# Values applied in one burst per group and tile, three rotating PSUM banks for exponentials and sums, a later tanh, and another order of the first y products

## The chip, the cores and the metric

The kernel runs on one core of a Trainium2 chip. The metric is the device time of one execution in microseconds (us). TensorE is called PE, its weight loads PEld, VectorE DVE, ScalarE ACT, GpSimd POOL; SyncE (SP) issues the transfers.

## The reference

Two blocks read the same `x` (2048 rows of 512): sliding-window attention with 32 heads of 16 and a window of 256, and a feed-forward block of width 1792 with a tanh gelu. A sigmoid gate mixes them row by row.

```python
g = _sigmoid((x * gate_w).sum(-1, keepdims=True))
# a: q, k, v = x @ wqkv; mask: 0 <= i - j < 256
p = _softmax(jnp.where(mask, (q @ k.T) * Dh ** -0.5, -1e9))
a = (p @ v) @ wo
# b
h = _gelu(x @ w1 + b1)
b = h @ w2 + b2
return g * a + (1 - g) * b
```

## The kernel before, in words

**Dense work.** The rows are cut into four tiles of 512 (T, NT = 4), each into four blocks of 128 (NB). Every dense product is done three times in fp32r (`mm3`, L94): high by high, high by low, low by high, with numbers split into a high part (rounded) and a low part (the rest). `qkv(t)` (L280) makes queries, keys and values of a tile and stores them in DRAM (SQ, SK, SV). `mlp(n)` (L569) is one of eight turns over half of the hidden width (`half`) and one tile: seven `u` products (12 matmuls each), `gelu` (L542) on each, then four `y` products (one per block, 21 matmuls each). Half 0 adds `b2` and stores into YA; half 1 reads YA back through the tile `ya` and stores into YB. `final(t)` (L631) multiplies by `wo` and mixes with the gate.

`gelu` has seven steps on a 128x512 tile: two ACT passes on `u` in PSUM, which give x1 = u + b1 and its square; f2 on DVE, the argument of tanh (L552); f3 on ACT, tanh (L555); f4 on DVE (L558); f5 on DVE, the high part of h (L561); f6 on POOL, the low part of h (L564). A `y` product's third matmul (L97) is the one that reads the low part. The tiles `x1` and `sq` have two buffers each.

**Attention.** Heads are taken in 8 groups of four (NG), keys in 16 blocks of 128 (NKB). A unit `u` is one key block of one group: 128 units. Three steps per head run beside each other:

- `att_max` (L374): scores `sm` of a query block, whose row maximum is taken by DVE (tile `jm`, L388), 8 units ahead (LEAD). `att_rows` (L394) turns the maxima of four blocks into two extra rows of `qs`, through the tiles `nm` and `tt`, with four POOL copies (`put`, L408).
- `att_exp` (L414): scores `st` of a key block against its up to 384 queries, in PSUM (two banks); ACT writes the exponentials into a tile `pt` (L435, 11 buffers, two heads each), POOL zeroes what the mask forbids (`sel`, L427 and L430).
- `att_pv` (L441): the values of a key block times those exponentials are added into the PSUM bank `pv` of a query tile `c`. A value operand is 32 columns wide, so the four heads of a group stand side by side in the array (`tile_position`, L455). It is in plain fp32, each of these matmuls being two instructions in the records. `att_pvs` (L473) calls it after every odd key block: for the two blocks done last, and after the second block of a tile also for the last two of the tile before, which reach into this tile. That makes two bursts per group and tile. After the second, ACT copies `pv` out as `nd` (L466), and it goes to DRAM.

`att_norm` (L485) then, for every second group, reads the denominators (`den`) and numerators (`num`) back, takes the reciprocal (`rec`, L496), spreads it through DRAM (`rb`) and multiplies (L501).

**What sets the order.** On PE, ACT, DVE and POOL the instructions stand as the program emits them (`MANUAL`), and every engine works through its own in that order. The program keeps a planned clock: `tick(ns)` advances it, `after(ns, f)` puts a step on a list that `tick` empties when it is due, `need` brings due steps forward. The main loop goes through the units; per head it emits, as `ORDER` says, `sm`, `st`, at the third head (PVAT) the `att_pvs` of the unit before, and then `fill`, which emits dense work worth STEP / 4 of planned time. So a `u` or `y` matmul group stands between two pairs of score matmuls. `GELU` lists the planned delays of f1 to f6, `NORM` the step of `att_norm`. Transfers all go through SP, whose order a scheduler chooses; SP waits in order as well.

A tile with a tag takes the next of that tag's `bufs` buffers, and its first writer waits until the last reader of the tile that was there is done.

Of the kernel before, what the change touches and what calls it, by code (L numbers as in the profile page):

```python
# [18 lines left out]
T = 512  # L19
# [13 lines left out]
def gated_mix(ctx: ExitStack, tc: tile.TileContext, x, wqkv, wo, w1, b1, w2, b2, gate_w, out):  # L33
# [35 lines left out]
    b2b = cp.tile([128, D], F32, name="b2b")  # L69
# [15 lines left out]
    nms = [cp.tile([128, RB, 32], F32R, name=f"nm{i}") for i in range(2)]  # L85
    for nm in nms:
        nc.gpsimd.memset(f32(nm), 0.0)
# [38 lines left out]
    def load_raw(key, early=False):  # L126
        kind, i = key
        src = {"qk": lambda: wk4[:, :, i * 128:(i + 1) * 128],
               "v": lambda: wqkv[i * 128:(i + 1) * 128, 2 * D:3 * D],
               "w1": lambda: w1k[:, :, i * 128:(i + 1) * 128],  # L130
               "w2": lambda: w2[i * 128:(i + 1) * 128],
               "wo": lambda: wo[i * 128:(i + 1) * 128]}[kind]()
        if early and kind == "v" and i < 2:
            raw = sb.tile([128, T], F32, tag="sq", bufs=2, name=f"raw_{kind}{i}")
        elif early and kind == "v":
            raw = f32(sb.tile([128, 2, T], F32R, tag="h", bufs=8, name=f"raw_{kind}{i}"))[:, 0]
        elif early:
            raw = sb.tile([128, 2, 384], F32, tag="pt", bufs=11, name=f"raw_{kind}{i}")
# [46 lines left out]
    def load_xr(t):  # L185
        for b in range(NB):
            xrs[t, b] = sb.tile([128, D], F32, tag="tmp", bufs=4, name=f"xr{t}_{b}")
            nc.sync.dma_start(xrs[t, b], x[t * T + b * 128:t * T + (b + 1) * 128])
# [38 lines left out]
    def gate_z(t, b):  # L227
        xr = xrs.pop((t, b))
        junk = sb.tile([128, D], BF16, tag="x1", bufs=2, name=f"xj{t}_{b}")
        nb = t * NB + b  # L230
        nc.vector.tensor_tensor_reduce(junk, xr, gwb, 1.0, 0.0, ALU.mult, ALU.add, z[:, nb:nb + 1])
# [48 lines left out]
    def qkv(t):  # L280
# [17 lines left out]
        for n, (kind, j) in enumerate(pieces):  # L298
# [9 lines left out]
            if t == 0 and n == 10:  # L308
                nc.sync.dma_start(b2b, b2.partition_broadcast(128))
                nc.sync.dma_start(b1c, b1.rearrange("(f p) -> p f", p=128))  # L310
# [83 lines left out]
    def att_rows(g_, rb):  # L394

        need(*[("max", g_, rb * RB + b, i) for b in range(RB) for i in range(4)])
        m = Ms.pop((g_, rb))
        nm = nms[rb % 2][:, :, 0:8].rearrange("p b (i k) -> p k b i", k=2)
# [3 lines left out]
        tt = sb.tile([128, RB, 32], F32, tag="tt", bufs=2, name=f"tt{g_}_{rb}")  # L402
        nc.vector.transpose(tt.rearrange("p b c -> p (b c)"), f32(nms[rb % 2]).rearrange("p b c -> p (b c)"))

        def put(i):
            dst = qs[96:104, :, rb * RB * 128:(rb + 1) * RB * 128]
            dst = dst.rearrange("r s (b i j) -> r s b i j", b=RB, i=4)[:, :, :, i]
            nc.gpsimd.tensor_copy(dst, tt[32 * i:32 * i + 8].unsqueeze(1).broadcast_to([8, 2, RB, 32]))  # L408
            if i == 3:
                done.add(("rows", g_, rb))  # L410
        for i in range(4):
            after(PUT * (i + 1), put, i)

    def att_exp(g_, kb, i):  # L414
# [3 lines left out]
        if s == 0:  # L418
            pts[g_, kb, pr] = sb.tile([128, 2, 384], F32, tag="pt", bufs=11, name=f"pt{g_}_{kb}_{pr}")
# [21 lines left out]
    def att_pv(g_, kb, c):  # L441
# [6 lines left out]
        if first:  # L448
# [3 lines left out]
            pvs[g_, c] = ps.tile([128, T], F32, tag="pv", bufs=1, name=f"pv{g_}_{c}")  # L452
# [7 lines left out]
        tick((e - q) * 1.67 + 150)  # L460
        if kb % NB == NB - 1 and c == kb // NB:
            nd = sb.tile([128, T], F32, tag="tmp", bufs=4, name=f"nd{g_}_{c}")
# [22 lines left out]
    def att_norm(t, c):  # L485
# [3 lines left out]
        rec = sb.tile([128, 32], F32, tag="rec", bufs=2, name=f"rec{t}_{c}")  # L489
        nc.sync.dma_start(den, v[:, 16, :].rearrange("i (j c) -> i j c", c=32))  # L490
        num = sb.tile([128, T], F32, tag="tmp", bufs=4, name=f"num{t}_{c}")
        rb = sb.tile([128, T], F32, tag="tmp", bufs=4, name=f"rb{t}_{c}")
        nc.sync.dma_start(num, v[:, 0:16, :])

        def rcp():
            nc.vector.reciprocal(rec, den)  # L496
            nc.sync.dma_start(RD[t][c].rearrange("h (j c) -> (h j) c", c=32), rec)
# [17 lines left out]
    def load_o(t):  # L515
# [7 lines left out]
        for c in range(NC):  # L523
            need(("o", t, c))
            if t == 0:
                raw = sb.tile([128, T], F32, tag=("x1", "sq")[c % 2], bufs=2, name=f"or{t}_{c}")
            else:
                raw = sb.tile([128, 2, 384], F32, tag="pt", bufs=11, name=f"or{t}_{c}")
# [40 lines left out]
    def mlp(n):  # L569
# [22 lines left out]
        for b in range(NB):  # L592
            ts = slice(b * 128, (b + 1) * 128)
            if n + 1 == len(TURNS) and b == 2:
                load_o(0)
            p = ps.tile([128, D], F32, tag="d", bufs=2, name=f"y{t}_{half}{b}")
            if half == 1:
                ya = sb.tile([128, D], F32, tag="ya", bufs=2, name=f"ya{t}_{b}")
                need(("y", 0, t, b))
                nc.sync.dma_start(ya, YA[t][ts])  # L600
            for i in range(HF):
                need(hs[i].name, ("w", ("w2", half * HF + i)))
                w = wt["w2", half * HF + i]
                mm3(p, hs[i][:, 0, ts], hs[i][:, 1, ts], w[:, 0], w[:, 1], i == 0, i == HF - 1)
                yield MM3
                if last and b == NB - 1 and later:
                    load(later.pop(0))
            def ev(p=p, b=b, ts=ts, ya=b2b if half == 0 else ya):
                y = sb.tile([128, D], F32, tag="y", bufs=1, name=f"yo{t}_{half}{b}")
                nc.vector.scalar_tensor_tensor(y, p, 0.5, ya, op0=ALU.mult, op1=ALU.add)  # L610
                nc.sync.dma_start((YA, YB)[half][t][ts], y)
                done.add(("y", half, t, b))
            after(100, ev)
# [17 lines left out]
    def final(t):  # L631
# [8 lines left out]
        for b in range(NB):  # L640
# [3 lines left out]
            a = sb.tile([128, 2, 384], F32, tag="pt", bufs=11, name=f"ao{nb}")  # L644
# [52 lines left out]
    for u in range(-LEAD, NU):  # L697
# [17 lines left out]
        if u % NB == 2 and -NB < u < NU - NB:  # L715
            att_load_v(*divmod(u // NB + 1, NT))
# [17 lines left out]
NORM = 6000  # L734
GELU = (700, 1500, 2300, 3300, 4200, 5000)
# [29 lines left out]
```

## Time and profile before

| | |
|---|---|
| runs | 807.09 us median of 3 (806.85 to 811.15) |
| profiled execution | 806.06 us, of which span 804.4 us |
| PE busy | 783.4 us, 97% |
| DVE, ACT, POOL busy | 526.3, 427.0, 357.9 us |
| `pv` matmuls (L455) | 1408 records, 91.4 us busy |
| `st`, `sm` matmuls | 172.2, 169.5 us busy |
| mean granted PE clock | 0.998 |
| transfers | 135.72 MB, 52.5% of 16 engines' time |

A matmul's record begins when it starts and ends when its last row is through; matmuls follow each other before that, so the distance from start to start says what one costs, and the busy times of neighbours overlap. An engine's waits are listed with the instruction that released it. In the rows, `L455` is line 455 of the kernel, `128x384` the partitions and elements of the operand, `x16` a run of 16 such records in one row.

### The profile page before, as it was taken

How to read it: one execution, taken by the hardware profiler on the slowest of the kernel's cores; microseconds unless marked ns; L12 is line 12 of the kernel's file. 1: busy time of each engine (PE TensorE's matmuls, PEld its weight loads, DVE VectorE, ACT ScalarE, POOL GpSimd, SP SyncE). 2: the span in 40 equal slices, each digit the busy share in tenths (PEclk: the TensorE clock that was granted, in tenths of full speed). 3: DMA queues.
4: the chain of work that ended last, by engine and by line, in shares of the span. 5: the costliest groups of instructions: out<-in, count | busy, mean ns of one | idle time of the engine just before them, and what ended most of it. 6: DMA issues, size and time to landing. Idle time of an engine off the chain costs nothing.

```text
span 804.4 us, 14522 instructions
## 1 busy us (share of the span) xinstructions
PE 783.4 (97%) x4630; PEld 612.9 (76%) x4630; DVE 526.3 (65%) x1517; ACT 427.0 (53%) x865; POOL 357.9 (44%) x702
## 2 busy tenths in 40 slices
PE   9999999989999999999999999999999999999988
PEld 6888888866777777777767867877787778776767
DVE  4532333997478757956895798568767966891353
ACT  4433423365467446745674576456646654775631
POOL 2200000156357544854674477437645753675100
PEclk9999999999999999999999999999999999999999
DMA  9985856636332544462235546432664374345863
GB/s 259 390 313 197 307 176 196 207 114 237 105 101 68 195 141 120 147 194 86 78 108 158 170 126 218 119 97 90 195 193 125 103 227 153 99 128 177 282 234 117
DMA packets 94925, 135.72 MB, mean 169 GB/s; under 512 B 32256, under 2 KB 43776, under 8 KB 94848
## 3 DMA queue, kind: packets, MB, share of 16 engines
q1 hardware_dynamic: 94848, 134.79, 52.5%
q8 instruction: 37, 0.61, 0.3%
q14 instruction: 40, 0.33, 0.1%
HBM read 79.70 MB, written 55.05 MB: 168 GB/s over the span
## 4 chain that ended last, share of the span: by engine, by line
PE 75%; DVE 12%; issue 4%; ACT 4%; POOL 3%; DMA 2%; SPq 0%; DVEq 0%; POOLq 0%; ACTq 0%
PE pv L455 9%; PE st L423 8%; PE sm L383 7%; PE y L95 6%; PE y L97 6%; PE y L96 5%; DVE jm L388 4%; PE u L95 4%; PE qk L95 4%; PE qk L97 4%; PE qk L96 4%; PE u L96 3%; PE u L97 3%; DVE sqh L552 2%; PE v L95 2%
## 5 line engine op out<-in xcount | busy, mean ns | idle before, releaser
L388 DVE CUSTOM_DVE_ANT_0 jm<-sm,mask 128x384 bf16<-128x384 f32 (+2 forms) x512 | 269.7, 527 | 129.7 <-PE sm L383 106.5
L435 ACT ACTIVATE pt<-st 128x384 f32<-128x384 f32 (+2 forms) x512 | 232.2, 471 | 194.8 <-PE st L423 189.6
L427 POOL TENSOR_SCALAR_AFFINE_SELECT pt<-pt 128x256 f32<-128x256 f32 x256 | 120.9, 472 | 203.9 <-ACT pt L435 199.3
L423 PE MATMUL st<-qs,ks 128*128 128x384 f32 (+2 forms) x512 | 172.2, 338 | 8.5 <-ACT pt L435 5.6
L383 PE MATMUL sm<-ks,qs 96*128 96x384 f32 (+2 forms) x512 | 169.5, 333 | 4.2 <-DVE M L388 4.0
L423 PEld LDWEIGHTS st<-qs,ks 128*128 128x128 f32 x512 | 97.2, 190 | 36.7 <-ACT pt L435 14.1
L383 PEld LDWEIGHTS sm<-ks,qs 96*128 96x128 f32 x512 | 96.4, 188 | 30.4 <-DVE M L388 8.9
L430 POOL TENSOR_SCALAR_AFFINE_SELECT pt<-pt 128x256 f32<-128x256 f32 x224 | 101.9, 455 | 0.0
L564 POOL TENSOR_TENSOR h<-x1h,h 128x512 fp32r<-128x512 f32 x56 | 75.4, 1346 | 42.3 <-DVE h L561 38.6
L455 PE MATMUL pv<-pt,vbuf 128*32 128x384 f32 (+2 forms) x1408 | 91.4, 388 | 0.1
L95 PE MATMUL y<-w,h 128*128 128x512 f32 x224 | 90.9, 406 | 0.0
L97 PE MATMUL y<-w,h 128*128 128x512 f32 x224 | 88.1, 393 | 0.9 <-POOL h L564 0.9
L96 PE MATMUL y<-w,h 128*128 128x512 f32 x224 | 87.8, 392 | 0.0
L408 POOL CAST qs<-tt 8x256 fp32r<-8x256 f32 x128 | 60.5, 473 | 50.5 <-PE u L97 39.2
L95 PE MATMUL u<-mx,w 128*128 128x512 f32 x196 | 80.5, 411 | 0.0
L96 PE MATMUL u<-mx,w 128*128 128x512 f32 x196 | 76.8, 392 | 0.0
L97 PE MATMUL u<-mx,w 128*128 128x512 f32 x196 | 76.6, 391 | 0.0
L455 PEld LDWEIGHTS pv<-pt,vbuf 128*32 128x32 f32 x1408 | 38.3, 109 | 36.9 <-issue 17.2
L555 ACT ACTIVATE sqh<-sqh 128x512 f32<-128x512 f32 x56 | 35.3, 631 | 46.5 <-DVE sqh L552 46.2
L552 DVE SCALAR_TENSOR_TENSOR sqh<-sqh,x1h 128x512 f32<-128x512 f32 x56 | 53.0, 946 | 2.3 <-ACT sqh L549 1.6
L250 DVE TENSOR_TENSOR qke<-qk,qke 128x512 fp32r<-128x512 f32 x32 | 22.1, 690 | 49.5 <-ACT qke L247 45.4
L95 PEld LDWEIGHTS y<-w,h 128*128 128x128 f32 x224 | 42.4, 189 | 11.8 <-issue 11.1
(118 smaller groups left out, 1186.2 us busy)
## 6 DMA issues: line engine op xcount, KB each, us to landing
mx<-XT SPq DMA_DIRECT2D x24, 512.0 KB
SQ<-qke SPq DMA_DIRECT2D x16, 512.0 KB
SK<-qke SPq DMA_DIRECT2D x16, 512.0 KB
qs<-SQ SPq DMA_DIRECT2D x64, 128.0 KB
ND<-nd SPq DMA_DIRECT2D x32, 256.0 KB
ks<-SK SPq DMA_DIRECT2D x60, 128.0 KB
raw_w<-in_B_w_dram SPq DMA_DIRECT2D x28, 256.0 KB
SV<-vx SPq DMA_DIRECT2D x16, 272.0 KB
```

Source lines behind the costliest of these rows:

```text
L95: nc.tensor.matmul(p, lh, rh, start=first, stop=False)
L96: nc.tensor.matmul(p, lh, rl, start=False, stop=False)
L97: nc.tensor.matmul(p, ll, rh, start=False, stop=last)
L383: nc.tensor.matmul(p[:, :w], qs[0:96, pr, b * 128:(b + 1) * 128], ks[0:96, pr, s, k0:k0 + w], start=True, stop=True)
L388: nc.vector.tensor_tensor_reduce(junk[:, :w], p[:, :w], mask[:, 384 - w:384], 1.0, -3e38, ALU.add, ALU.max, M[:, b % RB, i:i + 1])
L423: nc.tensor.matmul(p[:, :w], ks[:, pr, s, kb * 128:(kb + 1) * 128], qs[:, pr, kb * 128:kb * 128 + w], start=True, stop=True)
L427: nc.gpsimd.affine_select(out=pt[:, :, 0:128], in_=pt[:, :, 0:128], pattern=[[0, 2], [1, 128]], compare_op=ALU.is_ge, fill=0.0, base=0, ch ...
L430: nc.gpsimd.affine_select(out=pt[:, :, 256:384], in_=pt[:, :, 256:384], pattern=[[0, 2], [-1, 128]], compare_op=ALU.is_ge, fill=0.0, base= ...
L435: nc.scalar.activation(pt[:, s, :w], p[:, :w], AF.Exp, scale=SCALE)
L455: nc.tensor.matmul(pv[32 * i:32 * i + 32, q - c * T:e - c * T], vt[:, 68 * (kb % NB) + 17 * i:68 * (kb % NB) + 17 * i + 32], pts[g_, kb, i ...
L552: nc.vector.scalar_tensor_tensor(sq, sq, GC, x1, op0=ALU.add, op1=ALU.mult)
L564: nc.gpsimd.tensor_sub(h[:, 1], x1, f32(h[:, 0]))
```

## The change

1. `att_pvs` works once per group and tile, after the tile's last key block: on the six blocks that reach into the tile (four for the first tile). `pt` has 14 buffers, and a tile's values are fetched at the start of its first unit's turn and not two units earlier.
2. `pv` has no bank of its own. It takes one of three banks under the tag `st`, in turn with the scores. The planned cost of a value block falls from 1.67 ns per column and 150 to 0.8 and 40.
3. `GELU` puts f3 (tanh) at 3600 instead of 2300, and f4, f5, f6 at 4600, 5500 and 6800 instead of 3300, 4200 and 5000. `NORM` is 4500 instead of 6000.
4. The `y` products of the first two blocks are interleaved: six of block 0, three of block 1 (YSWAP), the last of block 0, the other four of block 1.
5. Buffers: `b2` is not kept but loaded into a `ya` tile for each `y` of half 0; `y` results use the tag `sq`; `nm` and `tt` have one buffer; the reciprocal is taken in place; `tmp` has three buffers, `raw` takes some of its tiles; the copy of the identity is gone; the first `v` weights are loaded into `xt`.

```diff
-    identr = cp.tile([128, 128], F32R, name="identr")
-    one = sb.tile([128, 128], F32, tag="x1", bufs=2, name="one")
-    make_identity(nc, one)
-    nc.vector.tensor_copy(identr, one)
-    ident = f32(identr)
+    ident = sb.tile([128, 128], F32, tag="x1", bufs=2, name="ident")
+    make_identity(nc, ident)
...
-        p = ps.tile([128, 384], F32, tag="st", bufs=2, name=f"st{g_}_{kb}_{i}")
+        p = ps.tile([128, 384], F32, tag="st", bufs=3, name=f"st{g_}_{kb}_{i}")
...
-            pvs[g_, c] = ps.tile([128, T], F32, tag="pv", bufs=1, name=f"pv{g_}_{c}")
+            pvs[g_, c] = ps.tile([128, T], F32, tag="st", bufs=3, name=f"pv{g_}_{c}")
...
-        tick((e - q) * 1.67 + 150)
+        tick((e - q) * 0.8 + 40)
...
         g_, kb = divmod(u, NKB)
-        if kb % 2 == 0:
-            return
         c, k = divmod(kb, NB)
-        blocks = [kb - 1, kb]
-        if k == 1 and c > 0:
-            blocks = [kb - 3, kb - 2] + blocks
-        for b in blocks:
-            att_pv(g_, b, c)
+        if k == NB - 1:
+            for b in range(max(kb - 5, 0), kb + 1):
+                att_pv(g_, b, c)
...
-            nc.vector.reciprocal(rec, den)
-            nc.sync.dma_start(RD[t][c].rearrange("h (j c) -> (h j) c", c=32), rec)
+            nc.vector.reciprocal(den, den)
+            nc.sync.dma_start(RD[t][c].rearrange("h (j c) -> (h j) c", c=32), den)
...
+        def y_start(b):
             if n + 1 == len(TURNS) and b == 2:
                 load_o(0)
+            ps_[b] = ps.tile([128, D], F32, tag="d", bufs=2, name=f"y{t}_{half}{b}")
+            ya = sb.tile([128, D], F32, tag="ya", bufs=2, name=f"ya{t}_{half}{b}")
+            if half == 0:
+                nc.sync.dma_start(ya, b2.partition_broadcast(128))
+            else:
                 need(("y", 0, t, b))
-                nc.sync.dma_start(ya, YA[t][ts])
+                nc.sync.dma_start(ya, YA[t][slice(b * 128, (b + 1) * 128)])
+            yas[b] = ya
+
+        def y_end(b):
+            ts = slice(b * 128, (b + 1) * 128)
+            y = sb.tile([128, D], F32, tag="sq", bufs=2, name=f"yo{t}_{half}{b}")
+            nc.vector.scalar_tensor_tensor(y, ps_[b], 0.5, yas[b], op0=ALU.mult, op1=ALU.add)
+            nc.sync.dma_start((YA, YB)[half][t][ts], y)
+            done.add(("y", half, t, b))
+
+        turns = [(0, i) for i in range(HF - 1)] + [(1, i) for i in range(YSWAP)] + [(0, HF - 1)]
+        turns += [(1, i) for i in range(YSWAP, HF)] + [(b, i) for b in range(2, NB) for i in range(HF)]
...
-        if u % NB == 2 and -NB < u < NU - NB:
-            att_load_v(*divmod(u // NB + 1, NT))
+        if u % NB == 0 and u >= 0:
+            att_load_v(*divmod(u // NB, NT))
...
-NORM = 6000
-GELU = (700, 1500, 2300, 3300, 4200, 5000)
+NORM = 4500
+YSWAP = 3
+GELU = (700, 1500, 3600, 4600, 5500, 6800)
```

Three places show how the order moves. The first is PE, at the values of group 0 and tile 1. `pv0_1` is the sum of that tile, `pt0_2_1` the exponentials of group 0, key block 2 and its second pair of heads; `x2` are the two heads of the pair. Before, the first burst comes while key block 6 is being scored:

```order
L423 MATMUL st0_6_2_2002<-qs_167,ks_168 128x384
L455 MATMUL pv0_1_2005<-pt0_2_0_1719,vbuf_162 32x128 x2
L455 MATMUL pv0_1_2005<-pt0_2_1_1754,vbuf_162 32x128 x2
L455 MATMUL pv0_1_2005<-pt0_3_0_1787,vbuf_162 32x256 x2
L455 MATMUL pv0_1_2005<-pt0_3_1_1829,vbuf_162 32x256 x2
L455 MATMUL pv0_1_2005<-pt0_4_0_1857,vbuf_162 32x384 x2
L455 MATMUL pv0_1_2005<-pt0_4_1_1881,vbuf_162 32x384 x2
L455 MATMUL pv0_1_2005<-pt0_5_0_1930,vbuf_162 32x384 x2
L455 MATMUL pv0_1_2005<-pt0_5_1_1958,vbuf_162 32x384 x2
L95 MATMUL y3_01_1945<-w2_4_1733,h3_4_1641 128x512
```

and the second one two units later, while key block 8 is being scored:

```order
L423 MATMUL st0_8_2_2118<-qs_167,ks_168 128x384
L455 MATMUL pv0_1_2005<-pt0_6_0_1981,vbuf_162 32x256 x2
L455 MATMUL pv0_1_2005<-pt0_6_1_2001,vbuf_162 32x256 x2
L455 MATMUL pv0_1_2005<-pt0_7_0_2042,vbuf_162 32x128 x2
L455 MATMUL pv0_1_2005<-pt0_7_1_2069,vbuf_162 32x128 x2
L95 MATMUL y3_02_2056<-w2_4_1733,h3_4_1641 128x512
```

Now all stands at the second place (`att_pv`'s line is 449 in the changed kernel):

```order
L449 MATMUL pv0_1_2100<-pt0_2_0_1709,vbuf_157 32x128 x2
L449 MATMUL pv0_1_2100<-pt0_2_1_1744,vbuf_157 32x128 x2
L449 MATMUL pv0_1_2100<-pt0_3_0_1763,vbuf_157 32x256 x2
L449 MATMUL pv0_1_2100<-pt0_3_1_1810,vbuf_157 32x256 x2
L449 MATMUL pv0_1_2100<-pt0_4_0_1837,vbuf_157 32x384 x2
L449 MATMUL pv0_1_2100<-pt0_4_1_1862,vbuf_157 32x384 x2
L449 MATMUL pv0_1_2100<-pt0_5_0_1923,vbuf_157 32x384 x2
L449 MATMUL pv0_1_2100<-pt0_5_1_1950,vbuf_157 32x384 x2
L449 MATMUL pv0_1_2100<-pt0_6_0_1973,vbuf_157 32x256 x2
L449 MATMUL pv0_1_2100<-pt0_6_1_1996,vbuf_157 32x256 x2
L449 MATMUL pv0_1_2100<-pt0_7_0_2019,vbuf_157 32x128 x2
L449 MATMUL pv0_1_2100<-pt0_7_1_2048,vbuf_157 32x128 x2
```

The matmuls are the same ones; the score of block 8 stands ahead of the burst in both kernels.

The second place is ACT, at the fourth hidden tile of the turn on row tile 0 (`h0_3`). Before, `x1h` and the square are followed by one exponential, the copy of `pv0_3`, and tanh (L555):

```order
L546 ACTIVATE x1h0_3_2588_2594<-u0_3_2523,b1c_139 128x512
L549 ACTIVATE sqh0_3_2588_2595<-u0_3_2523,b1c_139 128x512
L435 ACTIVATE pt1_0_1_2605<-st1_0_2_2606 128x384
L466 ACTIVATE nd0_3_2621<-pv0_3_2479 128x512
L555 ACTIVATE sqh0_3_2588_2595<-sqh0_3_2588_2595 128x512
L435 ACTIVATE pt1_0_1_2605<-st1_0_3_2631 128x384
```

Now (tanh is L544):

```order
L535 ACTIVATE x1h0_3_2568_2574<-u0_3_2501,b1c_136 128x512
L538 ACTIVATE sqh0_3_2568_2575<-u0_3_2501,b1c_136 128x512
L429 ACTIVATE pt1_0_1_2585<-st1_0_2_2586 128x384
L460 ACTIVATE nd0_3_2618<-pv0_3_2589 128x512
L429 ACTIVATE pt1_0_1_2585<-st1_0_3_2629 128x384
L544 ACTIVATE sqh0_3_2568_2575<-sqh0_3_2568_2575 128x512
```

One exponential has changed places with tanh.

The third place is PE, at the last hidden tile of the same turn (`h0_6`). Before, its product with block 0 (`y0_00`) follows that of `h0_5` at once:

```order
L97 MATMUL y0_00_2816<-w2_5_1780,h0_5_2747 128x512
L383 MATMUL sm1_13_3_2927<-ks_168,qs_167 128x384
L423 MATMUL st1_5_2_2931<-qs_167,ks_168 128x384
L95 MATMUL y0_00_2816<-w2_6_1849,h0_6_2810 128x512
L96 MATMUL y0_00_2816<-w2_6_1849,h0_6_2810 128x512
L97 MATMUL y0_00_2816<-w2_6_1849,h0_6_2810 128x512
```

Now three products of block 1 (`y0_01`) stand between; the third of them and what follows:

```order
L92 MATMUL y0_01_2935<-w2_2_1585,h0_2_2500 128x512
L377 MATMUL sm1_14_3_2979<-ks_163,qs_162 128x384
L417 MATMUL st1_6_2_2983<-qs_162,ks_163 128x384
L90 MATMUL y0_00_2803<-w2_6_1859,h0_6_2797 128x512
L91 MATMUL y0_00_2803<-w2_6_1859,h0_6_2797 128x512
L92 MATMUL y0_00_2803<-w2_6_1859,h0_6_2797 128x512
```

The low part of `h0_6` is wanted three products later than before.

More of the change, by code (lines that the diff above doesn't have):

```diff
@@ L84, in gated_mix @@
                                 fill=1.0, base=-k, channel_multiplier=1)
-    nms = [cp.tile([128, RB, 32], F32R, name=f"nm{i}") for i in range(2)]
-    for nm in nms:
-        nc.gpsimd.memset(f32(nm), 0.0)
+    nms = cp.tile([128, RB, 32], F32R, name="nm")
+    nc.gpsimd.memset(f32(nms), 0.0)
     vbuf = cp.tile([128, 2, NB * 68 + 16], F32, name="vbuf")
@@ L228, in gate_z @@
         xr = xrs.pop((t, b))
-        junk = sb.tile([128, D], BF16, tag="x1", bufs=2, name=f"xj{t}_{b}")
+        junk = sb.tile([128, D], BF16, tag="sq", bufs=2, name=f"xj{t}_{b}")
         nb = t * NB + b
@@ L591, in mlp @@
             load_x(TURNS[n + 1][1], f"mx{half}")
-        for b in range(NB):
-            ts = slice(b * 128, (b + 1) * 128)
+        ps_, yas = {}, {}
+        def y_start(b):
             if n + 1 == len(TURNS) and b == 2:
                 load_o(0)
-            p = ps.tile([128, D], F32, tag="d", bufs=2, name=f"y{t}_{half}{b}")
-            if half == 1:
-                ya = sb.tile([128, D], F32, tag="ya", bufs=2, name=f"ya{t}_{b}")
-                need(("y", 0, t, b))
[L600 to L613, printed above, removed]
@@ new lines, in mlp @@
+        turns = [(0, i) for i in range(HF - 1)] + [(1, i) for i in range(YSWAP)] + [(0, HF - 1)]
+        turns += [(1, i) for i in range(YSWAP, HF)] + [(b, i) for b in range(2, NB) for i in range(HF)]
+        for b, i in turns:
+            ts = slice(b * 128, (b + 1) * 128)
+            if i == 0:
+                y_start(b)
+            need(hs[i].name, ("w", ("w2", half * HF + i)))
+            w = wt["w2", half * HF + i]
+            mm3(ps_[b], hs[i][:, 0, ts], hs[i][:, 1, ts], w[:, 0], w[:, 1], i == 0, i == HF - 1)
+            yield MM3
+            if last and b == NB - 1 and later:
+                load(later.pop(0))
+            if i == HF - 1:
+                after(100, y_end, b)
```

35 lines of the change are left out of this document (16 added, 19 removed).

## Prediction

> **What bounds the kernel now.** I read the page first, then the table of windows, the waits, and the order of time around three places. The profiled execution took 806.06 us, of which 804.4 are the span; the median of the runs is 807.09 (806.85 to 811.15). The sum below is made against 806.06, and 807.09 - 806.06 = 1.0 us is added at the end for the median.
>
> ```profile
> PE 783.4 (97%) x4630; PEld 612.9 (76%) x4630; DVE 526.3 (65%) x1517; ACT 427.0 (53%) x865; POOL 357.9 (44%) x702
> 160.00:200.00 40.00, 35.69 (x186) 26.71 (x188) 35.93 (x97) 24.75 (x50) 24.91 (x40) 0.96 0.52 181
> ```
>
> The first row is the page's; the second is one stage of the table of windows (length, then busy time of PE, PEld, DVE, ACT and POOL, and the granted clock). PE is busy 97% of the span, and the most that it idles is 4.3 us between 160 and 200, where DVE is busy 90%. So two things count: PE time that does no work while it shows as busy, and PE's waits. For the first, PE's order of time (start, duration, operation) in an ordinary stretch and around three `pv` bursts:
>
> ```profile
> 253.20 0.34 PE L423 MATMUL st<-qs,ks 128*128 128x384 f32 x1
> 253.38 0.39 PE L95 MATMUL u<-mx,w 128*128 128x512 f32 x1
> 253.60 0.39 PE L96 MATMUL u<-mx,w 128*128 128x512 f32 x1
> ...
> 254.24 0.33 PE L423 MATMUL st<-qs,ks 128*128 128x384 f32 x1
> 254.50 1.50 PE L455 MATMUL pv<-pt,vbuf 128*32 128x384 f32 x16
> 255.93 0.50 PE L95 MATMUL u<-mx,w 128*128 128x512 f32 x1
> 256.26 0.40 PE L96 MATMUL u<-mx,w 128*128 128x512 f32 x1
> ...
> 263.18 0.86 PE L455 MATMUL pv<-pt,vbuf 128*32 128x256 f32 x16
> 263.97 0.50 PE L95 MATMUL y<-w,h 128*128 128x512 f32 x1
> ...
> 272.65 2.15 PE L455 MATMUL pv<-pt,vbuf 128*32 128x128 f32 x32
> 274.72 0.50 PE L95 MATMUL y<-w,h 128*128 128x512 f32 x1
> ```
>
> From first `pv` start to the next product: 0.79 us for blocks of 256+128 columns, 1.43 for 384+384, 2.07 for 128+256+384+384. Each 384 columns more cost 0.64, whether they come as one block or two, so 0.79 - 0.64 = 0.15 is paid per burst. From an `st` to the next start are 0.18 ordinarily, but 0.26 to a `pv` (0.08 more), and the product behind the burst takes 0.33 to the next start, not 0.22 (0.11 more). Fixed cost: 0.34 us a burst.
>
> For the waits, those of PE and of its weight loads, and the one behind them (who waited for whom: us in total, times, longest):
>
> ```profile
> ACT sqh L555 <- DVE sqh L552: 46.2, 41, 2.8
> PEld st L423 <- ACT pt L435: 14.1, 28, 1.5
> PEld sm L383 <- DVE M L388: 8.9, 14, 2.2
> PE st L423 <- ACT pt L435: 5.6, 11, 1.2
> PEld st L423 <- POOL qs L408: 5.2, 9, 1.2
> PE sm L383 <- DVE M L388: 4.0, 5, 1.8
> PEld y L97 <- POOL h L564: 2.6, 4, 0.7
> PEld pv L455 <- POOL pt L430: 1.1, 5, 0.3
> ```
>
> A PEld wait counts from the load before, which still ran under a matmul, so the time lost lies between the PE row and the PEld row. One case shows where, and how the whole stall comes about:
>
> ```profile
> 246.02 1.29 POOL L564 TENSOR_TENSOR h<-x1h,h 128x512 fp32r<-128x512 f32 x1
> 246.07 1.79 DVE L552 SCALAR_TENSOR_TENSOR sqh<-sqh,x1h 128x512 f32<-128x512 f32 x1
> 247.90 0.63 ACT L555 ACTIVATE sqh<-sqh 128x512 f32<-128x512 f32 x1 [1.46 <-DVE sqh L552]
> 248.96 0.19 PEld L423 LDWEIGHTS st<-qs,ks 128*128 128x128 f32 x1 [1.11 <-ACT pt L435]
> 248.96 0.44 PE L423 MATMUL st<-qs,ks 128*128 128x384 f32 x1 [0.79 <-ACT pt L435]
> ```
>
> The groups of the two VectorE operations that gelu does on whole tiles (busy us, mean ns, idle before):
>
> ```profile
> L552 DVE SCALAR_TENSOR_TENSOR sqh<-sqh,x1h 128x512 f32<-128x512 f32 x56 | 53.0, 946 | 2.3 <-ACT sqh L549 1.6
> L558 DVE SCALAR_TENSOR_TENSOR x1h<-sqh,x1h 128x512 f32<-128x512 f32 x56 | 38.9, 694 | 4.5 <-ACT sqh L555 3.0 <-POOL qs L408 1.5
> ```
>
> GpSimd's subtraction of one hidden tile runs while VectorE makes the tanh argument of the next (f2, L552). That one takes 1.79 us, where the like-shaped L558 has a mean of 0.69. ScalarE has come to the tanh and waits 1.46; the exponentials stand behind it, both `st` banks are full, and PE stops for a time between 0.79 and 1.11. So of 14.1 I take 9.6 as lost (28 times 0.16 less), of the 8.9 for `sm` 6, of the 5.2 for `qs` rows 3, of the 2.6 for `y` 1.6.
>
> **The change, part by part.** *Bursts.* Columns and matmuls stay; 64 bursts (2 per group and tile, 8 x 4 of these) become 32. Saved: 32 x 0.34 = 10.9, bounds 9 (if a long burst pays more inside) and 11.2. Before, both bursts of a tile waited at times for the last mask (1.1 us of weight loads); now four older blocks come first, so another 0.5 to 1.5: together **-12** (-9 to -13).
>
> *Tanh and third bank.* The planner's clock gives a unit 2296 of dense work plus 8 matmuls of 173: 3680 ns; a `u` (4 x 681) thus 4366. f6 at 5000 fell 634 behind the next `u`, ran 1.35 us (row of L564 in the next fence) and so covered f2 at 1500. At 6800 it falls at 2434 to 3784, between f2 and f4 (4600). And tanh stands 2100 behind f2 instead of 800; the mean wait was 46.2/41 = 1.13. One more `st` bank takes a further 0.5 us of delay. Of 9.6 I expect 2 to stay: **-7.5** (-4 to -10). `sm` waits (6) come from the same slow f2, and the stretched DVE time goes (56 x 0.25 = 14 us): **-2.5**, with bounds -6 and +3, since a 2.9 us burst leaves DVE only three `sm` banks to work off.
>
> *The clock after a stall.* One `sm` wait of 1.79 us at 165.58 was followed by matmuls at half speed; that is the 0.96 in the first window (4% of 40 us, 1.6 us lost):
>
> ```profile
> 165.58 0.44 PE L383 MATMUL sm<-ks,qs 96*128 96x384 f32 x1 [1.79 <-DVE M L388]
> L564 POOL TENSOR_TENSOR h<-x1h,h 128x512 fp32r<-128x512 f32 x56 | 75.4, 1346 | 42.3 <-DVE h L561 38.6 <-ACT w L150 3.3
> ```
>
> It is in the -2.5 with half its price. [...]
>
> *Rows, first products.* The `qs` rows are planned alike, with the longer burst ahead of them: -1 of 3 (0 to -2). The last hidden tile is wanted three products later, but made 1.8 us later: -1 of 1.6 (0 to -1.6). **-2.**
>
> *What it adds.* Sixteen loads of `b2` take the place of one, on the one queue through which all transfers go; `norm` is planned in steps of 4500 instead of 6000:
>
> ```profile
> 10.17 1.73 SPq L309 DMA_DIRECT2D b2b<-in_B_b_dram x1
> L600 SPq DMA_DIRECT2D ya<-YA x16: 422/442/635, 493.6 to 738.6; - x16
> 452.25 0.43 SPq L348 DMA_DIRECT2D qs<-SQ  x1
> 463.32 0.34 PE L383 MATMUL sm<-ks,qs 96*128 96x384 f32 x1
> 291.83 0.60 SPq L490 DMA_DIRECT2D den<-ND  x1
> 295.85 0.35 DVE L496 RECIPROCAL rec<-den 128x32 f32<-128x32 f32 x1
> ```
>
> A `b2` issue costs the queue 0.44 (as `ya`) to 1.73: 7 to 28 us over four feed-forward turns, four a turn. Behind each stand `den`, `num` and the next `ks` and `qs`. The `qs` loads have cover: the last one of a tile is issued 10.6 us before its `sm`. If 4 us of that went, 6.6 would be left, and PE waits for none. `den` has less: here 3.4 us from issue to the reciprocal, which sits in DVE's in-order queue, so all `sm` reductions stand behind it. Taking 1.5 to 3 us off leaves 0.4 to 1.9, and some reciprocals will wait. Also, at the first two `u` tiles x1's buffer comes free late, since f6 now ends as the next but one starts, and ScalarE waits for GpSimd there, with little but gelu behind it, as exponentials have hardly begun. `y` tile 2 takes tile 0's bank four products after that ends, where it had seven; an eviction is one pass like L558 (0.69), and four products are planned at 4366, so I cost that at nothing; with VectorE 3 us behind it would cost PE the rest. The values of a tile are fetched behind the burst of the tile before and wanted four units later, as they were. Together **+2.5** (0 to +8). The dropped identity copy is hidden behind the first x load: 0.
>
> Sum: -12 - 7.5 - 2.5 - 2 + 2.5 = -21.5, so 784.6 profiled and **785.5 us** as a median.
>
> **Rivals.** (1) *Only the bursts pay.* f2 does not escape: if VectorE runs 0.9 us behind the plan, f6 meets it again, or meets f4 and weight splits instead, and the stalls stay. Then -12, +2.5 and no more: 797.5. For it: f6's 75.4 us on GpSimd don't shrink. Against it: even a slow f2 has 1.3 us more before tanh is reached. [...]
>
> (2) *The bursts don't pay*: the fixed cost goes with the number of matmuls. Without the -12: 797.5. Against it: 16 more matmuls and 384 more columns cost the same 0.64 as 384 columns with none more.
>
> (3) *Norm waits.* If each of 16 reciprocals, or the product that follows, holds DVE for so long that PE loses 1 us, it is 16 more: 801.5, at the edge of no change. Against it: DVE shows no wait for a transfer there now.
>
> (4) *Slower: the shared bank.* `pv` now takes its bank from `st`. Two `st` after a burst, PE needs the bank which ScalarE still copies out. If gelu passes or a tanh stand ahead of that copy, PE stops at each of 32 bursts. The gains come to 24; to end 0.5% slower, 28/32 = 0.9 us a burst must go; at 1.2 it is 785.5 + 38 = 824.
>
> ```profile
> ACT nd L466 <- PE pv L455: 7.1, 22, 1.1
> ```
>
> Against it: in 22 of 32 bursts ScalarE stood idle at that copy, ahead of PE and not behind.
>
> **How the numbers follow.** Forecast 0.66; rival 1 0.18, rival 2 0.03, rival 3 0.08, rival 4 0.05. A measurement of this kernel can tell 0.5% (4 us) from no change: faster is below 803, slower above 811. Forecast and rivals 1 and 2 are faster (0.87), rival 3 half (0.04): 0.91; the other half is the same (0.04); rival 4 is slower (0.05). The range begins where all terms of the forecast come out at their better ends (-13, -10, -6, -3.6, 0: 774.5), and reaches up over rivals 1 and 2, to 798; rivals 3 and 4 are left out.
>
> **What would show it.** Right: 32 bursts of about 2.7 us start to start (2.07 for the first tile of a group); ACT's wait at tanh under 20 us; L552's mean near 0.75; the PEld wait `st` <- ACT under 4. Wrong: bursts of 3 us or more; DVE waiting for `den` or `rb`; PE waiting for the copy `nd`; PE busy under 97%. A time above 803 would mean that a new wait ate both gains.

## The result, and the profile after

The changed kernel takes **788.4 us** (786.97 to 789.78, five runs) against 807.09 before (805.88 to 811.15, five runs beside it). The ratio is 0.9757, with a 95% interval of 0.9728 to 0.9787. The profiled execution took 789.78, with a span of 788.1, so 16.3 of span went between the two profiles and 18.7 between the medians; 21.5 had been forecast.

Below are the page's first row, the groups of `pv` and of VectorE's operations on whole tiles (busy us, mean ns, idle before), and the waits (us, times, longest), all of the kernel after but for one row. Its line numbers are five to eleven lower than before: `sm` is L377, `st` L417, `pv` L449, f2 L541, tanh L544, f4 L547, f5 L550, f6 L553, the split of a weight L149, the third product L92.

```profile
PE 768.1 (97%) x4630; PEld 618.5 (78%) x4630; DVE 521.6 (66%) x1516; ACT 429.0 (54%) x865; POOL 363.6 (46%) x701
```

```profile
L449 PE MATMUL pv<-pt,vbuf 128*32 128x384 f32 (+2 forms) x1408 | 84.3, 386 | 0.0
L541 DVE SCALAR_TENSOR_TENSOR sqh<-sqh,x1h 128x512 f32<-128x512 f32 x56 | 46.7, 833 | 1.8 <-ACT sqh L538 1.6
L547 DVE SCALAR_TENSOR_TENSOR x1h<-sqh,x1h 128x512 f32<-128x512 f32 x56 | 42.0, 751 | 1.2 <-ACT sqh L544 1.2
L550 DVE CAST h<-x1h 128x512 fp32r<-128x512 f32 x56 | 27.2, 486 | 0.1
L149 DVE TENSOR_TENSOR w<-raw_w,w 128x512 fp32r<-128x512 f32 x28 | 24.2, 863 | 12.3 <-ACT w L145 12.3
```

The weight splits in the kernel before:

```profile
L154 DVE TENSOR_TENSOR w<-raw_w,w 128x512 fp32r<-128x512 f32 x28 | 23.1, 825 | 9.8 <-ACT w L150 9.7
```

The waits after:

```profile
ACT nd L460 <- PE pv L449: 57.9, 31, 2.5
...
PEld sm L377 <- DVE M L382: 19.5, 31, 2.2
...
ACT x1h L535 <- POOL h L553: 10.2, 5, 3.6
...
ACT sqh L544 <- DVE sqh L541: 8.9, 14, 1.9
...
DVE den L485 <- DMA den<-ND: 2.5, 1, 2.5
...
PEld st L417 <- ACT pt L429: 1.5, 2, 1.0
...
PEld st L417 <- POOL qs L402: 0.2, 1, 0.2
```

Three things are to be seen. ScalarE's wait at tanh fell from 46.2 to 8.9, and PE's weight loads for `st` hardly wait any more for the exponentials (14.1 to 1.5). But their waits for the row maxima, `sm` <- DVE, rose from 8.9 to 19.5. And f2 got faster (946 to 833 ns), while its like L547 and the weight splits got slower (694 to 751, 825 to 863). The copy of `pv` (nd) has ScalarE waiting ahead of it at 31 of 32 bursts.

PE's order of time around a burst of six blocks and one of a group's first tile, with four (start, duration, operation):

```profile
223.72 2.80 PE L449 MATMUL pv<-pt,vbuf 128*32 128x128 f32 x48
226.44 0.50 PE L90 MATMUL u<-mx,w 128*128 128x512 f32 x1
...
258.89 2.15 PE L449 MATMUL pv<-pt,vbuf 128*32 128x384 f32 x32
260.97 0.50 PE L90 MATMUL y<-w,h 128*128 128x512 f32 x1
```

From start to start a burst takes 226.44 - 223.72 = 2.72 us for six blocks and 2.08 for the four of a first tile; 2.7 and 2.07 had been forecast.

To add up what PE loses I took from both traces the distance from each product's start to the next, less the ordinary one (0.18 us behind a score product, 0.23 behind a dense one), wherever over 0.13 us was left. A stretch at half clock is in these sums too. By the product that came late:

| us lost | `st` | `sm` | `y` | all |
|---|---|---|---|---|
| before | 12.9 | 5.8 | 1.6 | 26.0 |
| after | 1.8 | 13.1 | 0.9 | 24.1 |

The bursts, from start to start and with what goes beyond the ordinary distance at both ends, took 99.5 us before and 88.4 after. So of the 16.3 the bursts are 11.1 and the waits 1.9; 3.3 are spread over smaller distances and were not attributed.

How one of the two longest of the new waits comes about (order of time, all engines; the brackets say how long the engine was idle, and who released it):

```profile
407.28 1.28 POOL L553 TENSOR_TENSOR h<-x1h,h 128x512 fp32r<-128x512 f32 x1
407.33 1.78 DVE L149 TENSOR_TENSOR w<-raw_w,w 128x512 fp32r<-128x512 f32 x1
...
409.03 0.89 DVE L541 SCALAR_TENSOR_TENSOR sqh<-sqh,x1h 128x512 f32<-128x512 f32 x1
...
409.84 0.54 DVE L382 CUSTOM_DVE_ANT_0 jm<-sm,mask 128x384 bf16<-128x384 f32 x1
...
410.45 0.44 PE L377 MATMUL sm<-ks,qs 96*128 96x384 f32 x1 [1.67 <-DVE M L382]
```

Here GpSimd's f6 meets a weight split and not f2. The split takes 1.78 us beside the group's mean of 0.86, f2 stands behind it, the maximum behind both, and PE waits 1.67 for an `sm` bank.

### The profile page after: what moved, and what is told of

The parts are those of the page before. It is cut to its first block, busy times and chain, and to the rows that moved or that the text cites. A ratio compares the mean times of both kernels' runs of the same rounds, so it can differ in the third digit from the quotient of the medians.

```text
span 788.1 us, 14535 instructions
## 1 busy us (share of the span) xinstructions
PE 768.1 (97%) x4630; PEld 618.5 (78%) x4630; DVE 521.6 (66%) x1516; ACT 429.0 (54%) x865; POOL 363.6 (46%) x701
## 4 chain that ended last, share of the span: by engine, by line
PE 66%; DVE 5%; issue 4%; DMA 2%; ACT 2%; POOL 1%; DVEq 0%; POOLq 0%; SPq 0%
PE pv L449 10%; PE st L417 9%; PE sm L377 9%; PE y L90 7%; PE y L91 6%; PE y L92 6%; PE u L90 5%; PE u L91 4%; PE u L92 4%; DVE jm L382 2%; PE a L92 1%; DVE sqh L541 1%; PE a L90 1%; PE a L91 1%; DMA ND<-nd 1%
## 5 line engine op out<-in xcount | busy, mean ns | idle before, releaser
L421 POOL TENSOR_SCALAR_AFFINE_SELECT pt<-pt 128x256 f32<-128x256 f32 x256 | 117.4, 459 | 184.0 <-ACT pt L429 177.9
L377 PE MATMUL sm<-ks,qs 96*128 96x384 f32 (+2 forms) x512 | 171.2, 336 | 8.7 <-DVE M L382 7.7
L417 PE MATMUL st<-qs,ks 128*128 128x384 f32 (+2 forms) x512 | 169.2, 332 | 0.9 <-ACT pt L429 0.9
L377 PEld LDWEIGHTS sm<-ks,qs 96*128 96x128 f32 x512 | 96.8, 189 | 37.5 <-DVE M L382 19.5
L417 PEld LDWEIGHTS st<-qs,ks 128*128 128x128 f32 x512 | 97.6, 191 | 18.7 <-ACT pt L429 1.5
L424 POOL TENSOR_SCALAR_AFFINE_SELECT pt<-pt 128x256 f32<-128x256 f32 x224 | 102.5, 457 | 0.0
L553 POOL TENSOR_TENSOR h<-x1h,h 128x512 fp32r<-128x512 f32 x56 | 81.8, 1460 | 37.2 <-DVE h L550 29.4
L402 POOL CAST qs<-tt 8x256 fp32r<-8x256 f32 x128 | 64.7, 505 | 50.7 <-PE u L92 38.8
L92 PE MATMUL y<-w,h 128*128 128x512 f32 x224 | 88.0, 393 | 0.0
L449 PE MATMUL pv<-pt,vbuf 128*32 128x384 f32 (+2 forms) x1408 | 84.3, 386 | 0.0
L92 PE MATMUL u<-mx,w 128*128 128x512 f32 x196 | 76.5, 390 | 0.0
L449 PEld LDWEIGHTS pv<-pt,vbuf 128*32 128x32 f32 x1408 | 41.5, 110 | 41.8 <-issue 29.1
L460 ACT ACTIVATE nd<-pv 128x512 f32<-128x512 f32 x32 | 19.2, 598 | 60.1 <-PE pv L449 57.9
L242 ACT ACTIVATE qke<-qk 128x512 fp32r<-128x512 f32 x32 | 19.2, 599 | 57.7 <-PE qk L92 43.1
L92 PEld LDWEIGHTS y<-w,h 128*128 128x128 f32 x224 | 42.3, 189 | 9.4
```

The source lines that it names most:

```text
L92: nc.tensor.matmul(p, ll, rh, start=False, stop=last)
L377: nc.tensor.matmul(p[:, :w], qs[0:96, pr, b * 128:(b + 1) * 128], ks[0:96, pr, s, k0:k0 + w], start=True, stop=True)
L417: nc.tensor.matmul(p[:, :w], ks[:, pr, s, kb * 128:(kb + 1) * 128], qs[:, pr, kb * 128:kb * 128 + w], start=True, stop=True)
L421: nc.gpsimd.affine_select(out=pt[:, :, 0:128], in_=pt[:, :, 0:128], pattern=[[0, 2], [1, 128]], compare_op=ALU.is_ge, fill=0.0, base=0, ch ...
L424: nc.gpsimd.affine_select(out=pt[:, :, 256:384], in_=pt[:, :, 256:384], pattern=[[0, 2], [-1, 128]], compare_op=ALU.is_ge, fill=0.0, base= ...
L449: nc.tensor.matmul(pv[32 * i:32 * i + 32, q - c * T:e - c * T], vt[:, 68 * (kb % NB) + 17 * i:68 * (kb % NB) + 17 * i + 32], pts[g_, kb, i ...
```

## The experiments

The question was where the forecast gains of the waits went, and which part earns what. In the expectations T is the prediction's theory: the later tanh and f6 take away the waits for exponentials. Against it stand B (the third bank does that, whenever tanh comes), L (the long burst brings the new `sm` waits) and C (VectorE simply has too much to do in some stretches, so PE waits at `sm` whatever is done for `st`). M is the fixed cost per burst, P that the `sm` waits come from VectorE's passes meeting GpSimd's. Each ratio is to the kernel before. "Lost" is the sum of the table above, made for that kernel's trace. Beside numbers 6, 9, 10 and 12 the kernel before took 805.98 us and not 807.09, so there a difference by ratios stands next to the one by times.

**1. The old times of gelu, all else as after.**

```diff
-GELU = (700, 1500, 3600, 4600, 5500, 6800)
+GELU = (700, 1500, 2300, 3300, 4200, 5000)
```

> The changed kernel with the planned delays of gelu as before (tanh at 2300, low part at 5000). Theory T, that the later tanh took the waits of the score matmuls for the exponentials (14.1 us of PEld waits before, 1.5 after): they come back to 8 or more, ScalarE waits again 35 us or more at tanh, and the time is 6 to 10 us above the changed kernel, 0.983 to 0.988 of before. Rival B, that the third bank took them: PEld waits stay under 4 and the time is within 3 us of the changed kernel.

Measured: 794.06 us, 0.9839 (0.9811 to 0.9867). Its waits:

```profile
ACT sqh L544 <- DVE sqh L541: 63.8, 46, 3.2
...
PEld sm L377 <- DVE M L382: 21.8, 32, 2.2
...
PEld st L417 <- ACT pt L429: 0.8, 3, 0.4
```

ScalarE waits at tanh even more than before the change (63.8 against 46.2), and still the loads for `st` wait only 0.8 us in all. So with a third bank these waits stay away whenever tanh comes, as B says; T isn't needed for them here (numbers 3 and 4 show what the later tanh does with two banks). B's time, within 3 us, did not come: the later times are worth 5.7 us with this order of `y`. What they take away is spread: `st` 3.6 to 1.8, `sm` 14.6 to 13.1, the last stage's `a` 5.7 to 3.6. Other products lose more, so that in all 2.8 us less are lost of the 4.8 between the two spans; the rest was not attributed.

**2 and 3. The burst and the bank apart.** Both give `pv` its own bank again and `st` two; number 2 also goes back to two bursts per group and tile, with the values fetched as before.

```diff
-        p = ps.tile([128, 384], F32, tag="st", bufs=3, ...
+        p = ps.tile([128, 384], F32, tag="st", bufs=2, ...
-            pvs[g_, c] = ps.tile([128, T], F32, tag="st", bufs=3, ...
+            pvs[g_, c] = ps.tile([128, T], F32, tag="pv", bufs=1, ...
```

Number 2 alone:

```diff
-        if k == NB - 1:
-            for b in range(max(kb - 5, 0), kb + 1):
+        if k % 2 == 1:
+            for b in range(max(kb - 3, 0) if k == 1 else kb - 1, kb + 1):
```

> The changed kernel with two value bursts per group and tile as before, the sum in a bank of its own and two banks for scores (a sum held over two units can't share the rotation); the fetch of the values as before. To be compared with the next kernel, which has the same banks and one burst. Theory M, a fixed 0.34 us a burst: 11 us above the next kernel, with waits of the row scores for VectorE as there. Rival L, that the long burst brought the waits for VectorE (19.5 us of PEld waits after, 8.9 before): those fall to about 9 here, and the difference is 4 us or less.

> The changed kernel with the sum of the values in a bank of its own and two banks for scores, one burst per group and tile. Theory T: with the later tanh two banks do nearly as well; 1 to 3 us above the changed kernel, PEld waits of the scores for the exponentials 3 to 5. Rival B: these waits come back to 10 or more, and the time is 6 to 10 us above the changed kernel. The other way: the shared bank costs something, and this is faster by 1 to 2 us.

Measured: 807.02 us, 1.0001 (0.9982 to 1.002), with two bursts; 789.67, 0.9779 (0.9759 to 0.98), with one. The waits for banks, of two bursts first:

```profile
PEld sm L377 <- DVE M L382: 18.4, 25, 1.6
...
PEld st L417 <- ACT pt L429: 7.5, 14, 2.4
```

```profile
PEld sm L377 <- DVE M L382: 13.5, 22, 1.9
...
PEld st L417 <- ACT pt L429: 10.0, 18, 2.4
```

One burst instead of two is worth 17.4 us: 11.8 in the bursts with their ends (100.4 to 88.7 us), and 5.2 less lost in waits (28.3 to 23.1). L is refuted: with two short bursts the `sm` waits were longer, not shorter. With two bursts and the banks of before, all the rest of the change is worth nothing. And the shared bank is worth 1.3 us, within what two such comparisons can tell. The `st` waits without it are those of B (10.0), the time is that of T: the bank changes which product waits (`st` loses 6.7 without it and 1.8 with it, `sm` 8.6 and 13.1).

**4. The late times alone, in the kernel before.**

```diff
-GELU = (700, 1500, 2300, 3300, 4200, 5000)
+GELU = (700, 1500, 3600, 4600, 5500, 6800)
```

> The kernel before with nothing changed but the planned delays of gelu (tanh at 3600, low part at 6800). Theory T: the PEld waits of the scores for the exponentials fall from 14.1 to 5 or less, those of the last hidden tile's product do not fall, since the order of the y products is the old one (they rise to 4 to 8 us), and the time is 3 to 7 us less than before, 0.991 to 0.996. Rival B: no change within 2 us, or slower by the waits for the hidden tiles.

Measured: 811.66 us, 1.0055 (1.0037 to 1.0073): slower. ScalarE's wait at tanh fell to 14.1, and `st` lost 6.7 us and not 12.9, so with two banks the later tanh takes away about half of that, as T has it in part (the loads still wait 8.2 for the exponentials, not 5 or less). But the last hidden tiles now come too late for the first `y` product:

```profile
ACT sqh L555 <- DVE sqh L552: 14.1, 17, 2.2
...
PEld y L97 <- POOL h L564: 7.0, 6, 2.0
...
PEld y L95 <- DVE h L561: 3.0, 3, 1.4
```

`y` lost 9.0 us where it had lost 1.6.

**5. The products of `y` in the plain order, all else as after.**

```diff
-YSWAP = 3
+YSWAP = 0
```

> The changed kernel with the y products of the first two blocks one after the other (the last hidden tile wanted three products earlier). Late tanh alone on the kernel before cost 9.0 us between starts at the y products. Theory: the same waits come back here, 6 to 10 us between starts, and the time is 5 to 9 us above the changed kernel. Rival: there they came with the two bursts, and here the time is within 2 us.

Measured: 800.69 us, 0.9929 (0.9905 to 0.9952).

```profile
PEld y L92 <- POOL h L553: 9.1, 8, 1.7
...
PEld y L90 <- DVE h L550: 4.7, 5, 1.5
```

The order is worth 12.3 us, more than the 5 to 9 of the theory; `y` loses 11.8 without it, the same wait as in number 4.

**6. Both undone.**

```diff
-YSWAP = 3
-GELU = (700, 1500, 3600, 4600, 5500, 6800)
+YSWAP = 0
+GELU = (700, 1500, 2300, 3300, 4200, 5000)
```

> The changed kernel with both the old planned delays of gelu and the y products in order. With one of the two undone it took 5.7 us (old delays) and 12.3 us (in order) more. Theory, the two belong together: the late tanh makes the hidden tile 1.8 us later, and the other order only pays that back. Then undoing both costs about what the old delays cost alone, 5 to 8 us above the changed kernel, with under 3 us between starts at the y products. Rival, each pays by itself: 15 us or more above.

Measured: 795.34 us, 0.9858 (0.9837 to 0.9879). With after and numbers 1 and 5 this is a square: neither 795.3, the order alone 794.1, the late times alone 800.7, both 788.4. `y` lost 2.7, so the waits at the hidden tile are mostly gone, as the theory has it. The two are one edit in truth, worth 6.9 us by the times and 8.2 by the ratios; late times alone cost 5.4, the order alone is worth 1.3 (5.7 and 1.5 by the ratios).

**7. f6 on VectorE.** No pass of gelu is left on GpSimd for VectorE to meet.

```diff
-            nc.gpsimd.tensor_sub(h[:, 1], x1, f32(h[:, 0]))
+            nc.vector.tensor_sub(h[:, 1], x1, f32(h[:, 0]))
```

> The changed kernel with the low part of the hidden tile (f6) subtracted by VectorE and not by GpSimd. Theory P, that the waits of the row scores which are left (19.5 us of PEld waits) come from GpSimd's subtraction holding VectorE up: the tanh argument's mean goes from 0.83 us to 0.75 or less, no weight split takes over 1.2 us any more, and these waits fall to 10 us or less, the time by 3 to 7 us. Rival C, that VectorE simply has too much to do: with 56 x 0.69 = 39 us more work there the waits rise to 25 us or more and the time by 3 us or more.

Measured: 794.46 us, 0.9845 (0.9829 to 0.9862). A group and the waits:

```profile
L541 DVE SCALAR_TENSOR_TENSOR sqh<-sqh,x1h 128x512 f32<-128x512 f32 x56 | 43.7, 781 | 0.9 <-ACT sqh L538 0.8
L149 DVE TENSOR_TENSOR w<-raw_w,w 128x512 fp32r<-128x512 f32 x28 | 20.6, 736 | 11.3 <-ACT w L145 11.3
```

```profile
PEld sm L377 <- DVE M L382: 30.1, 48, 1.6
```

The meetings cost VectorE's passes less: f2's mean goes from 833 to 781 ns, that of the weight splits from 863 to 736; after the change six f2 took 1.1 to 1.8 us. But VectorE is busy for 543.8 us and not 521.6, and PE's waits for it rise from 19.5 to 30.1. VectorE's load outweighs the meetings here: C.

**8. The low parts of 28 weights on GpSimd.**

```diff
-        after(LAND, split, key, nc.vector)
+        after(LAND, split, key, nc.gpsimd)
```

> The changed kernel with the low parts of the later weights (28 subtractions, 24.2 us on VectorE) made by GpSimd. Rival C: VectorE has 24 us less to do, the waits of the row scores fall to 12 us or less, the time by 3 us or more. Theory P: each of the 28 on GpSimd (about 1.3 us) holds VectorE's passes with two inputs up in its turn, the waits stay within 4 us of 19.5 and the time within 2 us.

Measured: 788.77 us, 0.9783 (0.9753 to 0.9813): the same as after.

```profile
L541 DVE SCALAR_TENSOR_TENSOR sqh<-sqh,x1h 128x512 f32<-128x512 f32 x56 | 51.2, 915 | 5.8 <-ACT sqh L538 5.5
L547 DVE SCALAR_TENSOR_TENSOR x1h<-sqh,x1h 128x512 f32<-128x512 f32 x56 | 47.1, 842 | 2.8 <-ACT sqh L544 2.8
```

```profile
PEld sm L377 <- DVE M L382: 13.3, 21, 1.4
...
PEld st L417 <- ACT pt L429: 6.1, 5, 2.7
```

VectorE's busy time falls to 510.9, by 10.7 and not by 24, as f2's mean rises to 915 ns and L547's to 842. The `sm` waits fall as C has it, nearly (13.3, not 12 or less), the time stays as P has it: `sm` loses 9.1 us and not 13.1, `st` 7.4 and not 1.8.

**9. f5 on ScalarE.** The high part of h is made there, and VectorE is rid of the 27.2 us of L550.

```diff
-            nc.vector.tensor_copy(h[:, 0], x1)
+            nc.scalar.activation(h[:, 0], x1, AF.Copy)
```

> The changed kernel with the high part of the hidden tile (f5, 56 passes, 27.2 us on VectorE) made by ScalarE. Theory C, that the row scores wait because VectorE has too much to do in each stretch: 27 us less there, their PEld waits fall from 19.5 to 12 or less; 56 x 0.6 = 35 us more on ScalarE bring some waits for the exponentials (3 to 8), and the time is 0 to 4 us less. Theory P, that they wait because of GpSimd's subtraction holding VectorE: they stay above 16, and the time within 2 us or above.

Measured: **781.39 us**, 0.9688 (0.9664 to 0.9713), better than both kernels. The page's row, a group, and the waits:

```profile
PE 762.4 (98%) x4630; PEld 616.0 (79%) x4630; DVE 494.9 (64%) x1460; ACT 452.5 (58%) x921; POOL 355.3 (46%) x701
```

```profile
L541 DVE SCALAR_TENSOR_TENSOR sqh<-sqh,x1h 128x512 f32<-128x512 f32 x56 | 45.3, 808 | 7.0 <-ACT sqh L538 6.7
```

```profile
ACT h L550 <- DVE x1h L547: 16.3, 19, 2.8
...
PEld sm L377 <- DVE M L382: 12.7, 23, 1.3
...
PEld st L417 <- ACT pt L429: 1.8, 3, 1.0
```

The meetings are about as many (808 ns beside 833), VectorE has 26.7 us less to do, and the waits at `sm` fall by a third (19.5 to 12.7) while those of `st` for exponentials stay low (1.5 to 1.8), though ScalarE now waits 16.3 us for VectorE. In all 16.5 us are lost and not 24.1, 7.6 less; the gain is 7.0 us by the times and 5.6 by the ratios, more than the 0 to 4 expected. Some 2.9 of the 7.6 are the half clock, as this trace holds no stretch of it within the span (granted clock 1.0, and 0.995 after). This is the clearest case for C.

**10. The third bank given to the row maxima.** `pv` shares four `sm` banks; `st` has two.

```diff
-        p = ps.tile([128, 384], F32, tag="sm", bufs=3, ...
+        p = ps.tile([128, 384], F32, tag="sm", bufs=4, ...
-        p = ps.tile([128, 384], F32, tag="st", bufs=3, ...
+        p = ps.tile([128, 384], F32, tag="st", bufs=2, ...
-            pvs[g_, c] = ps.tile([128, T], F32, tag="st", bufs=3, ...
+            pvs[g_, c] = ps.tile([128, T], F32, tag="sm", bufs=4, ...
```

> The changed kernel with the eighth bank under the tag of the row scores: these and the sum of the values take turns in four banks, the scores have two. Theory C: a bank more buys the row scores one VectorE pass of delay (0.6 us), their PEld waits fall from 19.5 to 10 or less, those of the scores for the exponentials rise from 1.5 to 6 to 10 (10.0 with two banks and an own bank for the sum), and the time is within 3 us of the changed kernel.

Measured: 787.35 us, 0.9756 (0.9732 to 0.978): the same as after, with the waits the other way round.

```profile
PEld st L417 <- ACT pt L429: 14.7, 22, 3.0
...
PEld sm L377 <- DVE M L382: 2.6, 5, 1.0
```

`sm` and `st` together lose 13.5 us here, 14.9 after, and 15.4 with the bank kept apart (number 3): the bank decides where PE waits, and not by much how long.

**11. The planned cost of the values as before.** It moves the due times of everything behind a burst.

```diff
-        tick((e - q) * 0.8 + 40)
+        tick((e - q) * 1.67 + 150)
```

> The changed kernel with the planned cost of a value block as before (1.67 ns a column and 150), which is nearer to what it takes. The matmuls stay as they are, only what the planned clock makes due moves ahead by up to 2 us after each burst. Theory: it shifts which pass meets which and no more, within 2 us of the changed kernel. Rival: the low figure is what keeps steps off the burst, and this is 3 us slower or more.

Measured: 788.6 us, 0.9768 (0.9749 to 0.9787): no difference to be seen.

**12. `norm` in its old steps.**

```diff
-NORM = 4500
+NORM = 6000
```

> The changed kernel with att_norm planned in steps of 6000 as before. My sum put about 1.5 us on the shorter step, as a wait of VectorE for den (it shows 2.5 us of that, once). If so: the wait goes and the time is 0.5 to 2 us less. Rival: the waits fall where PE has nothing to lose, within 1 us; or the shorter step helps the end of the kernel and this is slower.

Measured: 792.0 us, 0.982 (0.9796 to 0.9843). The one wait for `den` is gone, but `sm` loses 14.9 us and not 13.1, `a` 4.5 and not 3.6. The intervals of the two ratios just miss each other (0.9787 and 0.9796), so the shorter step looks worth something (3.6 us by the times, 5 by the ratios), and there is no sign that it costs anything.

## Why the prediction was right, and where a step failed

**Bursts (-12): right.** Each is as long as forecast, the bursts with their ends took 11.1 less, and numbers 2 and 3 show 11.8 with the rest held equal. That 17.4 came of it there was not in the sum: 5.2 less was lost in waits. Why fewer and longer bursts make fewer waits was not tried apart, nor one burst alone in the kernel before. Rival 2 is refuted by this pair.

**Tanh and third bank (-7.5): more, and with the weights the other way round.** `st` lost 11.1 less. The forecast put the later tanh first and let the bank add half a us of delay. With two banks the later tanh brings 12.9 down to 6.7 (number 4; 6.7 again in number 3). With three banks `st` loses 3.6 though ScalarE's stop at tanh is back in full (number 1; its loads wait 0.8 for exponentials and 3.8 for `qs` rows), and 1.8 with both. So either does the larger part, and the bank does more. As time it earned little: the bank is worth 1.3 us (number 3), since what left `st` came back at `sm`.

**`sm` (-2.5, bounds -6 and +3): this is the step that failed.** It became +7.3, outside its bounds. The forecast took the `sm` waits to come from the slow f2 alone. f2 did grow faster by 56 x 0.113 = 6.3 us of the 14 reckoned with, and 3.1 and 1.1 of these came back at L547 and the weight splits, as rival 1 has it. Numbers 7 and 9 show what lies under it: PE waits where VectorE has too much work in hand. That before, while PE was held at `st`, VectorE caught up, and that with the hold gone PE comes to `sm` sooner and waits there, is an inference. Numbers 3 and 10, which move the bank back and forth, bear it out, number 3 for 4.5 of the 7.3. It can't be all: with two bursts and the old banks (number 2) `st` still lost 8.5 and `sm` already 12.3. Which of the remaining edits brought that stays open; undone one by one, the planned cost, the step of `norm` and the times of gelu left `sm` at 11.1 to 14.9.

**Rows and first products (-2): right as a difference, wrong as a price.** The `qs` row waits went from 5.2 to 0.2, and `y` lost 0.9 and not 1.6. But the new order isn't an item of -1: it pays for the later f6. Left out beside the late times it costs 12.3 (number 5), and the late times without it cost 5.4 there and 4.5 in the kernel before (numbers 6 and 4). The forecast counted f6's 1.8 us of delay and the three products that cover it, but priced only the difference.

**The additions (+2.5).** Rivals 3 and 4 did not come: VectorE waited for `den` once, for 2.5 us, and ScalarE for `pv`; the trace shows no wait of PE for the copy `nd`. The price on `norm`'s shorter step had the wrong sign, as far as number 12 can tell. ScalarE waited 10.2 us for x1's buffer, at the third to seventh tile of the first turn, where two tiles had been forecast. The sixteen loads of `b2` held the queue for 0.35 to 0.50 us each, 0.44 in the middle, so the lower end of the forecast's 0.44 to 1.73. What either cost PE was not measured apart and stays open.

**The clock.** Half its price before was to be saved; within the span the after trace holds two whole stretches at half clock instead of one, half of 3.41 us each, so some 3.4 us lost and not 1.7.

Together: bursts -11.1, `st` -11.1, `sm` +7.3, `y` -0.7 and the small distances -3.3 come to -18.9, less what was lost more at the start and in the last stage (+0.8 `xp`, +0.8 `a`, +0.9 `u`), which is the 16.3. The forecast of 785.5 was 2.9 too low, and luck had a part in that: `sm` gave 9.8 less than forecast, and against it stood `st`, with 2.6 more than the 8.5 for its exponentials and rows, and the small distances, with 3.3 for which there was no term.

## What to carry to other kernels

When PE waits now for one engine and now for another, add both sums before a bank or a delay is moved: a bank moved from one to the other nearly leaves the sum as it was (13.5, 14.9 and 15.4 us here). What lowered the waits here was work taken off the engine that is short of time (6 to 7 us of the kernel's time for one pass moved to ScalarE; none for a pass moved to GpSimd, which slowed others down, f2 from a mean of 833 to 915 ns), and one long burst in place of two short ones (5.2 us less lost in waits). Where a stage is delayed, look for the first reader of its last output, and change that reader's order in the same edit. A fixed cost per switch of the kind of product, read from distances between starts, was the most reliable term here (0.34 us a burst, 10.9 for 32 of them; 11.1 came).

## What the runs showed of the hardware

The clock halved after short waits, and not after each of them. Each whole stretch at half clock lasts 3.41 us in the trace's record of the clock: one before, from 166.70, and two after, from 166.28 and 412.05. PE's order of time at the second of after, behind the wait of 1.67 us quoted above:

```profile
411.98 0.57 PE L90 MATMUL y<-w,h 128*128 128x512 f32 x1
412.35 0.63 PE L91 MATMUL y<-w,h 128*128 128x512 f32 x1
412.77 0.63 PE L92 MATMUL y<-w,h 128*128 128x512 f32 x1
```

From start to start a dense product takes 0.42 us, not 0.23. At the first stretch two waits of 0.83 and 0.86 us, 1.8 apart, went ahead; yet a wait of 1.78 later on is followed by products at full speed:

```profile
702.91 0.44 PE L377 MATMUL sm<-ks,qs 96*128 96x384 f32 x1 [1.78 <-DVE M L382]
...
703.60 0.39 PE L91 MATMUL y<-w,h 128*128 128x512 f32 x1
703.83 0.39 PE L92 MATMUL y<-w,h 128*128 128x512 f32 x1
```

From start to start these take 0.23 us, at a granted clock of 1.00 from 702.91 to 706. So waits of 0.83 and 0.86 us, of 1.67 and, before, of 1.79 had a stretch behind them and one of 1.78 had none. What decides it was not shown.
